# Layer 1's third and fourth PSUM bank as tiles of a pool of their own

## The chip, the core and the metric

The kernel runs on one core of a Trainium2 chip. A core has engines that work side by side, each through its own queue in order: TensorE (PE in the profile; its weight loads are PEld), VectorE (DVE), ScalarE (ACT), GpSimd (POOL) and SyncE (SP), which here issues transfers and reads a few values. TensorE writes its results to PSUM, a memory of eight banks of 128 partitions x 2 KB (512 float32 in each partition); VectorE and ScalarE read them from there into the larger memory SBUF. Engines wait for each other by semaphores, which the compiler of the kernel language sets: where a program takes a tile from a pool and writes it, the write waits until the readers of what lay there before are done.

The metric is the device time of one execution in microseconds (us), as the median of several runs.

## What is computed

Attention over windows (8 batches, 8 heads, 576 positions, 64 wide), and on its output a mixture of 16 experts in 4 groups. For each of 4,608 tokens one expert is chosen:

```python
x = attn_out.transpose(0, 2, 1, 3).reshape(B * S, H * D)     # 4608 x 512
g_idx = np.argmax(x @ w_group, axis=1)                       # group, then expert in the group
...
h = np.maximum(xg[mask_e] @ w1[g, e], 0.0)                   # layer 1: 512 -> 1024
ye = h @ w2[g, e]                                            # layer 2: 1024 -> 512
out[tok_idx] = combined[:, None] * ye
```

Inputs are float32. The change concerns the product `xg @ w1` of the experts, called layer 1 here.

## The kernel before, in words

The kernel works in two stages. Attention and the routing of tokens come first, in 36 steps of a hand-written software pipeline (the loop at L875). The experts follow, from some 184 us on. The order of the instructions on TensorE, ScalarE, VectorE and SyncE is the order of the program text (`manual_schedule`, L874); from L1057 on GpSimd's is too.

**Experts.** Experts are ranked by their number of tokens. Each gets a fixed number of slots (`CAPS`), split into pieces: three early pieces of 128, 128 and 256 slots, for which the tokens of the first batches suffice (the function `early`), and then 16 pieces, one per expert, of 192, 152, 368, 304, 304, 304, 296, 288, 272, 264, 256, 256, 248, 240, 216 and 192 slots (the loop at L1063). For each piece:

- *Gather and spread.* GpSimd gathers the rows of the piece's tokens (L690, tiles `xr`), one piece ahead. TensorE transposes them (`pt`, L721), ScalarE makes a float16 high part `xh` (L722) and VectorE the rest `xl` (L723). This runs between the matmuls of the piece before.
- *Layer 1* (`layer1`, L736). The 1,024 hidden columns are done in eight blocks of 128, `f` = 0 to 7. A block is 12 matmuls into one PSUM bank: 4 parts of the inner dimension, each with three products of float16 parts (weights high x `xh`, high x `xl`, low x `xh`). ScalarE then reads the bank and writes `hh`, the float16 of its positive part (L750), and VectorE reads the bank and writes the rest `hl` (L751).
- *Layer 2* (`layer2`, L759). For every 128 slots, 24 matmuls into a bank `y` (L802): for each of the eight blocks in order `hh` x high, `hl` x high, `hh` x low. In the middle of a tile stand transposes of the next piece. ScalarE scales the result (L776), GpSimd scatters it to the output (L763). A last tile of at most 64 slots is split into groups of columns; its slots are found by the small matmul `rp` (L666, after block 3), with VectorE's `entq` and ScalarE's `csq` behind it.
- *Weights.* The weights come as float32 in chunks of 512 KB through SyncE's queue (L611). ScalarE makes a chunk's high part (L625), VectorE its low part (L622). There are two sets of weights: while one expert works with one, the chunks of the next go into the other. Four chunks are done during layer 2 of a piece, the others during layer 1 of the following one, between the blocks, in the same queues of ScalarE and VectorE as `hh` and `hl`.
- Where no chunk is due, VectorE does a step of a table for tokens beyond the slots (`overflow`, tiles named `xT` in the profile), from 333 us to about 408 us.

**PSUM.** The eight banks are: psS with two tiles of one bank (attention's scores, later `a`), psT with two (transposes, `rp`), psA with one tile of two banks (attention's P times V, `o`), psX and psR with one bank each (layer 2's `y` in turn). Layer 1 takes its bank from `new_a` (L729). During attention that is always a psS tile. After attention (`att.close()`, L930) one last tile of two banks, `second`, is taken from psA and kept to the end (L942); the list `more_a` (L943) makes `new_a` give in turn the first half of `second`, a psS tile, the second half of `second`, a psS tile. So the even blocks of a piece write `second` and the odd ones `a`. A psS tile is handed out anew for every block; `second` is one tile for all blocks.

Of the kernel before, what the change touches and what calls it, by code (L numbers as in the profile page):

```python
# [8 lines left out]
F32 = mybir.dt.float32  # L9
# [6 lines left out]
PSUM = bass.MemoryType.PSUM  # L16

P = 128
# [46 lines left out]
def moe_attention_kernel(ctx, tc, q, k, v, cmask, wgate, wpack, out):  # L65
    nc = tc.nc
    pool = lambda name, bufs=1, **kw: ctx.enter_context(tc.tile_pool(name=name, bufs=bufs, **kw))
    cp = pool("cp")
    dram = pool("dram", space=bass.MemoryType.DRAM)
    psS = pool("psS", 2, space=PSUM)  # L70
    psT = pool("psT", 2, space=PSUM)
    psA = pool("psA", 1, space=PSUM)
    psX = pool("psX", 1, space=PSUM)
    psR = pool("psR", 1, space=PSUM)

# [19 lines left out]

    att = ExitStack()
    apool = lambda name, bufs=1, **kw: att.enter_context(tc.tile_pool(name=name, bufs=bufs, **kw))
    vp = apool("vp", NV)
    qp = apool("qp", NQ)
    kr = apool("kp").tile([P, 2, 2 * NK, 8, 32], F32, name="kr")  # L100
# [623 lines left out]
                xl[:, :, t * P : t * P + n], pt[:, :, 0:n], xh[:, :, t * P : t * P + n], ALU.subtract  # L724
            )

    more_a = []

    def new_a():  # L729
        if more_a:  # L730
            more_a.append(more_a.pop(0))
            if more_a[0] is not None:
                return more_a[0]
        return psS.tile([P, 512], F32, name="a", tag="s")

    def layer1(w, xs, cap, new_h):  # L736
        xh, xl = xs
        hh, hl = hs[:] = new_h()
        for f in range(8):
            a = new_a()  # L740
            mm = [(ww, xx, c) for c in range(4) for ww, xx in ((w[0], xh), (w[0], xl), (w[1], xh))]
            for i, (ww, xx, c) in enumerate(mm):
                nc.tensor.matmul(  # L743
                    a[:, 0:cap],
                    ww[:, c * FF + f * P : c * FF + f * P + P],
                    xx[:, c, 0:cap],
                    start=(i == 0),
                    stop=(i == len(mm) - 1),
                )
            nc.scalar.activation(hh[:, f, 0:cap], a[:, 0:cap], AF.Relu)  # L750
            nc.vector.scalar_tensor_tensor(  # L751
                hl[:, f, 0:cap], a[:, 0:cap], 0.0, hh[:, f, 0:cap], ALU.max, ALU.subtract
            )
            yield
# [184 lines left out]
    def new_h():  # L939
        return fh.tile([P, 8, CMAX], F16, name="hh"), fh.tile([P, 8, CMAX], F16, name="hl")  # L940

    second = psA.tile([P, 2, 512], F32, name="second", tag="o")  # L942
    more_a[:] = [None, second[:, 0], None, second[:, 1]]  # L943
    spare = xT[NBP - 1].rearrange("p c b i -> p (c b i)")
    taken = [0]

# [238 lines left out]
```

## Time and profile before

| | |
|---|---|
| median of 3 runs | 672.78 us (669.76 to 676.31) |
| the profiled execution | 663.49 us, of which the span from the first to the last instruction is 661.7 us |
| mean granted TensorE clock | 0.959 |
| busy share of the span | TensorE 89%, weight loads 62%, VectorE 61%, ScalarE 50%, GpSimd 38% |
| transfers | 127.53 MB, mean 193 GB/s |

By stages, the profile's windows say:

| us | what | TensorE busy | VectorE busy | ScalarE busy | clock | DMA share |
|---|---|---|---|---|---|---|
| 0 to 184 | attention | 147.90 | 135.19 | 98.35 | 0.94 | 0.75 |
| 184 to 234 | end of routing, early pieces | 40.91 | 25.12 | 21.55 | 0.83 | 0.25 |
| 234 to 272 | third early piece, first expert | 38.00 | 18.59 | 15.36 | 1.00 | 0.41 |
| 272 to 448 | the pieces of 152 to 296 slots | 160.60 | 111.62 | 86.74 | 0.98 | 0.62 |
| 448 to 573 | 288 to 256 slots | 120.70 | 72.95 | 69.75 | 0.99 | 0.66 |
| 573 to 662 | the last pieces | 80.03 | 41.97 | 39.84 | 0.98 | 0.43 |

How to read the rows of the profile: a row of the timeline has its start and its duration in us, the engine, the line of the kernel, the operation, what it writes `<-` what it reads, shapes, and in brackets how long its engine had been idle before it and what ended that (`<-`). `128*128 128x304` is a matmul with 128 x 128 weights and 304 columns. A row of the waits names the waiting engine and tile, what it waited for, the total in us, how often, and the longest. In the chain of waits each row has a start, a length and what it is; `x12` are twelve instructions merged. "issue" is idle time for which the profile shows no cause, "remote" the end of a wait whose origin it doesn't show.

### The profile page before, as it was taken

Reading aid. Unit: us, or ns where it says so; the run is one execution under the profiler, and the core shown is the slowest. Engines: PE = TensorE matmul, PEld = TensorE weight load, DVE = VectorE, ACT = ScalarE, POOL = GpSimd, SP = SyncE. Lnnn points to the kernel's source line nnn. Section 1 sums busy time; section 2 is a strip of 40 time slices with the busy share of each in tenths; the row PEclk is TensorE's granted clock in tenths of the full one; section 3 lists DMA queues with packets and bytes.
Section 4 is the critical chain, followed back from the end, with each engine's and each line's share of the span. In section 5 each row is a group of like instructions: output and inputs, shape, how many; then the busy total and the mean of one; then the engine's idle time right before and its main releaser. Section 6 shows DMA issues by size and latency. Waiting matters only on the chain.

```text
span 661.7 us, 18758 instructions
## 1 busy us (share of the span) xinstructions
PE 588.1 (89%) x7636; PEld 407.9 (62%) x7636; DVE 405.4 (61%) x849; ACT 331.6 (50%) x662; POOL 249.2 (38%) x304
## 2 busy tenths in 40 slices
PE   5898799878577999879989899898999999999896
PEld 4666576556464677655556566555576577667764
DVE  6765875887834672457485777554556567575720
ACT  2455565665532643456354455454557556556521
POOL 5874554539040171415142333414154134213311
PEclk9899989898796999979999999999999999999999
DMA  7887867796551026557565656656585677678300
GB/s 260 277 280 232 258 199 224 244 333 225 164 183 37 25 72 238 192 162 245 162 189 194 181 181 207 195 163 208 157 267 193 193 259 226 236 234 266 94 27 28
DMA packets 47916, 127.53 MB, mean 193 GB/s; under 512 B 7224, under 2 KB 8126, under 8 KB 47826
## 3 DMA queue, kind: packets, MB, share of 16 engines
q1 hardware_dynamic: 40466, 105.31, 50.0%
q0 software_dynamic: 7360, 20.98, 9.3%
q8 instruction: 62, 1.02, 0.6%
q14 instruction: 28, 0.23, 0.1%
HBM read 107.38 MB, written 19.24 MB: 191 GB/s over the span
## 4 chain that ended last, share of the span: by engine, by line
PE 57%; DVE 5%; issue 5%; ACT 3%; another core or an unknown queue 1%; POOL 0%; POOLq 0%; ACTq 0%
PE y L802 29%; PE second L743 12%; PE a L743 11%; PE pt L721 3%; DVE hl L751 1%; ACT hh L750 1%; PE lg_ps L389 1%; ACT wa1h L625 1%; ACT wa2h L625 1%; DVE wb1l L622 1%; PE lt_ps L378 0%; DVE wa1l L622 0%; DVE mv L492 0%; ACT wb2h L625 0%
## 5 line engine op out<-in xcount | busy, mean ns | idle before, releaser
L690 POOL DMA_INDIRECT xr<-xd,sent x80 | 96.5, 1206 | 33.2 <-issue 22.2
L763 POOL DMA_INDIRECT out<-yr,sent x30 | 30.0, 1001 | 204.6 <-ACT yr L776 180.8
L802 PEld LDWEIGHTS <-hh 128*128 128x128 f16 (+10 forms) x960 | 67.8, 99 | 59.8 <-issue 4.8
L743 PEld LDWEIGHTS <-wa1h 128*128 128x128 f16 x640 | 59.3, 98 | 25.7 <-issue 14.2
L723 DVE TENSOR_TENSOR xl<-pt,xh 128x512 f16<-128x512 f32 (+10 forms) x42 | 24.8, 595 | 77.7 <-ACT xh L722 69.0
L743 PEld LDWEIGHTS <-wb1h 128*128 128x128 f16 x576 | 55.9, 100 | 24.0 <-issue 13.2
L776 ACT ACTIVATE yr<-y,cs 128x512 f32<-128x512 f32 (+3 forms) x30 | 20.6, 688 | 91.7 <-PE y L802 67.4
L751 DVE SCALAR_TENSOR_TENSOR hl<-second,hh 128x256 f16<-128x256 f32 (+11 forms) x68 | 29.0, 427 | 55.6 <-ACT hh L750 41.4
L802 PE MATMUL y<-wb2h,hh 128*128 128x512 f16 (+6 forms) x272 | 60.6, 307 | 0.5 <-issue 0.5
L802 PE MATMUL y<-wb2h,hl 128*128 128x512 f16 (+6 forms) x272 | 60.4, 305 | 0.3
L802 PE MATMUL y<-wb2l,hh 128*128 128x512 f16 (+6 forms) x272 | 60.2, 305 | 0.5 <-issue 0.5
L802 PE MATMUL y<-wa2h,hl 128*128 128x512 f16 (+7 forms) x208 | 56.8, 330 | 0.1
L802 PE MATMUL y<-wa2h,hh 128*128 128x512 f16 (+7 forms) x208 | 56.9, 331 | 0.0
L127 POOL TENSOR_SCALAR vs<-vt 32x520 f32<-32x520 f32 x72 | 47.9, 665 | 23.8 <-DMA vt<-v 13.0
L802 PE MATMUL y<-wa2l,hh 128*128 128x512 f16 (+7 forms) x208 | 56.7, 330 | 0.0
L131 POOL TENSOR_SCALAR vs<-vt 32x520 f32<-32x520 f32 x64 | 41.9, 654 | 35.9 <-PE o L309 32.7
L802 PEld LDWEIGHTS <-hl 128*128 128x128 f16 (+10 forms) x480 | 35.0, 100 | 26.3 <-issue 1.2
L743 PE MATMUL second<-xh,wb1h 128*128 128x256 f16 (+6 forms) x144 | 39.6, 277 | 12.1 <-DVE hl L751 11.0
L750 ACT ACTIVATE hh<-a 128x256 f16<-128x256 f32 (+11 forms) x68 | 26.3, 387 | 42.9 <-PE a L743 22.0
L751 DVE SCALAR_TENSOR_TENSOR hl<-a,hh 128x256 f16<-128x256 f32 (+11 forms) x68 | 28.9, 425 | 30.1 <-ACT hh L750 19.2
L274 PE MATMUL s<-kr,qb 128*32 128x128 f32 x1152 | 43.3, 294 | 4.5 <-DMA kr<-k 2.2
L274 PEld LDWEIGHTS s<-kr,qb 128*32 128x32 f32 x1152 | 32.5, 117 | 18.0 <-issue 13.8
(201 smaller groups left out, 1552.5 us busy)
## 6 DMA issues: line engine op xcount, KB each, us to landing
w<-wpack SPq DMA_DIRECT2D x128, 512.0 KB
vt<-v SPq DMA_DIRECT2D x36, 260.0 KB
qb<-q SPq DMA_DIRECT2D x36, 256.0 KB
xd<-x SPq DMA_DIRECT2D x72, 128.0 KB
kr<-k SPq DMA_DIRECT2D x34, 256.0 KB
xr<-xd,sent POOLq DMA_INDIRECT x80
kr<-k SPq DMA_DIRECT2D x4, 128.0 KB
out<-yr,sent POOLq DMA_INDIRECT x30
```

What stands on the lines that cost most here:

```text
L127: nc.gpsimd.tensor_scalar(vs[n][even], vt[n][even], 1.0, 1.0, ALU.mult, ALU.mult)
L131: nc.gpsimd.tensor_scalar(vs[n][odd], vt[n - 1][odd], 1.0, 1.0, ALU.mult, ALU.mult)
L274: nc.tensor.matmul(s[32 * j : 32 * j + 32, c].rearrange("p w k -> p (w k)"), qv[:, (sl * 2 + a) * 32 : (sl * 2 + a) * 32 + 32], kr[:, :, k ...
L690: nc.gpsimd.indirect_dma_start(out=xr[:, 256 * h : 256 * h + 256], out_offset=None, in_=xd[0:known].rearrange("n (h c) -> (n h) c", h=2), ...
L721: nc.tensor.transpose(pt[:, c, 0:n], xr[0:n, c * P : c * P + P], id32[0:n, 0:n])
L723: nc.vector.tensor_tensor(xl[:, :, t * P : t * P + n], pt[:, :, 0:n], xh[:, :, t * P : t * P + n], ALU.subtract)
L743: nc.tensor.matmul(a[:, 0:cap], ww[:, c * FF + f * P : c * FF + f * P + P], xx[:, c, 0:cap], start=(i == 0), stop=(i == len(mm) - 1),)
L750: nc.scalar.activation(hh[:, f, 0:cap], a[:, 0:cap], AF.Relu)
L751: nc.vector.scalar_tensor_tensor(hl[:, f, 0:cap], a[:, 0:cap], 0.0, hh[:, f, 0:cap], ALU.max, ALU.subtract)
L763: ins = nc.gpsimd.indirect_dma_start(out=out.rearrange("n (g c) -> (n g) c", g=g), out_offset=bass.IndirectOffsetOnAxis(ap=at, axis=0), in ...
L776: nc.scalar.activation(yr[0:n, :], yp[0:n, :], AF.Copy, scale=cs[0:n, t : t + 1])
L802: nc.tensor.matmul(yp[P // g * j : P // g * j + n, 0 : DM // g], h[:, f, t * P : t * P + n], ww[:, f * DM + DM // g * j : f * DM + DM // g ...
```

## The change

psA becomes a pool of the attention stage (`apool`), so that its two banks are given back at `att.close()`. In its place a new pool psB is opened at that point, with two tiles of one bank each. `reuse_waits="tile"` lets a tile of the new pool wait only for the last use of the memory under that tile, as for the other pools opened there. `more_a` becomes a list of pools, and `new_a` takes a fresh tile in turn from psB and psS. The order of the four banks (psB, psS, psB, psS) is that of before, and no instruction is added to or taken from the text of an engine's work. In the profile the tiles of both pools are named `a`.

```diff
     psT = pool("psT", 2, space=PSUM)
-    psA = pool("psA", 1, space=PSUM)
     psX = pool("psX", 1, space=PSUM)
...
     apool = lambda name, bufs=1, **kw: att.enter_context(tc.tile_pool(name=name, bufs=bufs, **kw))
+    psA = apool("psA", 1, space=PSUM)
     vp = apool("vp", NV)
...
-    more_a = []
+    more_a = [psS]
 
     def new_a():
-        if more_a:
-            more_a.append(more_a.pop(0))
-            if more_a[0] is not None:
-                return more_a[0]
-        return psS.tile([P, 512], F32, name="a", tag="s")
+        more_a.append(more_a.pop(0))
+        return more_a[0].tile([P, 512], F32, name="a", tag="s")
...
-    second = psA.tile([P, 2, 512], F32, name="second", tag="o")
-    more_a[:] = [None, second[:, 0], None, second[:, 1]]
+    more_a[:] = [psS, pool("psB", 2, space=PSUM, reuse_waits="tile")]
```

## The prediction

> **What bounds the kernel now.** I read the chain of work first, then the waits of TensorE, then the timeline around those waits. The page gives span and chain:
>
> ```profile
> span 661.7 us, 18758 instructions
> PE 57%; DVE 5%; issue 5%; ACT 3%; another core or an unknown queue 1%; POOL 0%; POOLq 0%; ACTq 0%
> PE y L802 29%; PE second L743 12%; PE a L743 11%; PE pt L721 3%; DVE hl L751 1%; ACT hh L750 1%; PE lg_ps L389 1%; ACT wa1h L625 1%; ACT wa2h L625 1%; DVE wb1l L622 1%; PE lt_ps L378 0%; DVE wa1l L622 0%; DVE mv L492 0%; ACT wb2h L625 0%
> ```
>
> TensorE's matmuls of the expert layers (`second`, `a`, `y`) carry more than half of the chain, so a gap on TensorE there is time of the kernel. The view of waits, for PE alone, says which gaps there are (total us, times, longest):
>
> ```profile
> PE second L743 <- DVE hl L751: 18.9, 11, 4.8
> ...
> PE a L743 <- issue: 2.5, 3, 1.1
> ```
>
> The longest entry is layer 1 waiting to write a bank of `second` until VectorE has read one. `a`, the same matmuls into the other two banks, has no wait on VectorE or ScalarE in this list. The timeline of one of the eleven places, in the piece of 304 slots that begins at 360.6 us, shows which reader it waits for:
>
> ```profile
> 368.65 0.29 PE L743 MATMUL a<-xh,wa1h 128*128 128x304 f16 x1
> 368.95 0.42 ACT L750 ACTIVATE hh<-a 128x304 f16<-128x304 f32 x1 [3.10 <-PE second L743]
> 369.41 0.47 DVE L751 SCALAR_TENSOR_TENSOR hl<-a,hh 128x304 f16<-128x304 f32 x1 [1.77 <-issue]
> ...
> 370.07 0.29 PE L743 MATMUL a<-xh,wa1l 128*128 128x304 f16 x1
> ...
> 372.38 0.47 DVE L751 SCALAR_TENSOR_TENSOR hl<-second,hh 128x304 f16<-128x304 f32 x1 [0.67 <-ACT hh L750]
> ...
> 372.90 0.29 PE L743 MATMUL second<-xh,wa1h 128*128 128x304 f16 x1 [2.54 <-DVE hl L751]
> ...
> 376.00 0.38 PE L802 MATMUL y<-wa2h,hh 128*128 128x512 f16 x1
> ...
> 377.13 0.47 DVE L751 SCALAR_TENSOR_TENSOR hl<-a,hh 128x304 f16<-128x304 f32 x1
> ```
>
> Number the eight blocks of layer 1 f0 to f7: f0 and f4 write the first half of `second`, f2 and f6 the second half, the odd ones two psS tiles in turn. Block f6 starts at 372.90, 0.05 us after `hl` of f4 ended (372.38 + 0.47 = 372.85). But f4 used the other half; the last reader of f6's own half, `hl` of f2, was before all these rows. So a write to either half waits for the reads of both: `second` is two banks but behaves as one buffer that must be empty two blocks back. The psS tiles don't: f5 (`a`) starts at 368.65, before `hl` of f3 (the other psS tile) has even begun at 369.41.
>
> **The change part by part.**
>
> *Two tiles in place of two halves.* Each bank now has its own last reader, so a block waits for the `hl` four blocks back instead of two. In the piece above f6 then needs f2 only, and starts when f5 ends, at 370.07 + 0.29 = 370.36, so the whole 2.54 us goes. Block f7 needs f3's `hl`, done at 369.41 + 0.47 = 369.88, and does not wait either. The 11 waits together are 18.9 us. The largest of the others:
>
> ```profile
> 284.97 0.28 PE L743 MATMUL second<-xh,wb1h 128*128 128x152 f16 x1 [4.81 <-DVE hl L751]
> 342.77 0.29 PE L743 MATMUL second<-xh,wb1h 128*128 128x304 f16 x1 [2.60 <-DVE hl L751]
> 430.81 0.29 PE L743 MATMUL second<-xh,wa1h 128*128 128x296 f16 x1 [2.69 <-DVE hl L751]
> 461.09 0.40 PE L743 MATMUL second<-xh,wb1h 128*128 128x288 f16 x1 [3.14 <-DVE hl L751]
> ```
>
> *The clock.* The two longest waits cost more than their length. The chain in order of time (start, us, what) has the same work before and after them, and the windows their granted clock (behind the count of PE's instructions: PEclk, DMA share, GB/s):
>
> ```profile
> 273.22 0.79 PE second L743 x12
> 274.01 0.79 PE a L743 x12
> ...
> 284.97 1.68 PE second L743 x12
> 286.64 1.52 PE a L743 x12
> 288.16 3.53 PE y L802 x12
> 292.13 2.60 PE y L802 x12
> 448.68 1.47 PE second L743 x12
> 461.09 3.04 PE second L743 x12
> ```
>
> ```profile
> 284.97:288.16 3.19, 3.19 (x25) 0.50 0.58 189
> 461.09:465.61 4.52, 4.52 (x25) 0.68 0.79 226
> ```
>
> After the 4.81 us wait the clock is 0.50, and the work takes 1.68 + 1.52 + 3.53 - 0.79 - 0.79 - 2.60 = 2.55 us more; after the 3.14 us wait 3.04 - 1.47 = 1.57 us more. Without these pauses the clock stays up: 4.1 us.
>
> *What is late next.* ScalarE and VectorE don't become faster; TensorE only stops waiting for them there, and next meets their results in layer 2, which reads `hh` and `hl` block by block (three of its 24 matmuls for each, 2.60/12 = 0.217 us a matmul). In the 304 piece layer 2 starts 2.54 us earlier, at 373.5, and needs `hl` of f7 at its 23rd matmul, 373.5 + 22 x 0.217 = 378.2. VectorE has it at 377.13 + 0.47 = 377.6, even if it gains nothing: covered, by 0.6 us. The other places of the same size have the same order of work. The piece at 284.97 is short (152 slots) and not covered:
>
> ```profile
> 284.83 1.22 DVE L622 SCALAR_TENSOR_TENSOR wa2l<-w,wa2h 128x1024 f16<-128x1024 f32 x1
> ...
> 285.96 0.31 DVE L751 SCALAR_TENSOR_TENSOR hl<-a,hh 128x152 f16<-128x152 f32 x1
> ```
>
> Here `hl` of f5 ends at 285.96 + 0.31 = 286.27 and doesn't depend on f6. Behind them VectorE has `hl` of f6 (0.31), a weight chunk (1.22) and `hl` of f7 (0.31): 288.1. Layer 2's first tile then ends two matmuls later, at 288.6, and with the transposes in its middle (292.13 - 288.16 - 3.53 = 0.44) at 289.0; before it ended at 292.13 + 2.60 = 294.7. So this piece gains 5.7, not 4.81 + 2.55 = 7.4: 1.7 us come back as waits in layer 2.
>
> *Transfers and queues.* No DMA and no instruction of ScalarE, VectorE, GpSimd or SyncE is moved; all follow TensorE earlier. The pieces around the big waits use less of the DMA engines than later ones that run without a wait:
>
> ```profile
> 418.00:448.00 30.00, 27.31 (x210) 17.68 (x209) 15.48 (x30) 14.58 (x24) 9.07 (x9) 1.00 0.61 188
> 573.00:594.00 21.00, 21.00 (x151) 15.52 (x150) 13.72 (x24) 12.73 (x20) 6.81 (x6) 1.00 0.77 245
> ```
>
> 30 us shortened by 2.7 raises the share from 0.61 to 0.67, below the 0.77 at which TensorE is busy 21.00 of 21.00 us. Weights cost nothing more.
>
> *The pool's move.* PSUM still holds eight banks, and the new pool takes the two that attention gives back, at the point where `second` took them. Its first write waits for attention's last P times V result to be read, as `second` did: 0. Handing tiles over per block adds a release for some 76 blocks (half of 19 runs of layer 1 with 8 each). The psS tiles pay that already, and `a` has 2.5 us of issue idle in all, before 3 of its blocks: bounds 0 and 2.5; I take 0, as the other blocks of `a` show no gap.
>
> *Sum.* 18.9 + 4.1 - 1.7 = 21.3 us. The profiled execution took 663.5 us (span 661.7 and 1.8 around it), so it would take 642.2. The median of the runs, 672.8, lies 9.3 above it, and the trace doesn't show where; I carry the 21.3 us over unchanged: 651.5.
>
> That more buffering of results pays is not sure by itself. The Trainium skill, TensorE: Matmul & The Clock Gate, section HAM oscillation, tells of a kernel where PSUM double-buffering brought no further gain once the loop was in order. By that result the sum is 0 and the time 672.8; by the wait rows it is 21.3. I go by the rows, since there every wait ends 0.05 us after a read of the wrong bank; the rule's case is the first rival.
>
> **The rivals.**
>
> *The waits move into layer 2.* ScalarE and VectorE decide, and TensorE waits for `hl` of f4 to f7 at `y` instead. For it: the margin in the 304 piece is only 0.6 us, and the short piece already pays 1.7. Against it: by the sums above the large pieces are covered. It decides where `hl` of f7 comes over 0.6 us later than now. If half of the 21.3 comes back, the time is 672.8 - 10.7 = 662; if all of it, or if the new tiles still wait for each other, 672.8.
>
> *The late evacuations belong to this execution.* In the 304 piece ScalarE idles 3.10 us before `hh` of f3, though f3's matmuls had ended before 368.65, and no row says why. If other executions don't have this, the waits of 4.81, 2.54, 2.69 and 3.14 us (13.2) aren't there to be saved. Left are 18.9 - 13.2 = 5.7 us, of which the 2.60 has a visible cause: 672.8 - 5.7 gives 667. Against it: the four lie in four pieces, always before f6, and even the fastest run without the profile (669.8) took longer than the profiled one, not less.
>
> *The handover costs TensorE a bubble per block (slower).* If a released tile brings a second wait instruction before each of its blocks, all 76 of those blocks pay it. It turns the gain into a loss of 1% from (21.3 + 6.7)/76 = 0.37 us per block. At 0.4 us it gives 672.8 - 21.3 + 30.4 = 682. Against it: the `a` blocks are such tiles and show 2.5/76 = 0.03 us.
>
> **How the numbers follow.** One per cent, 6.7 us, is about what a measurement of this kernel can tell from no change. Forecast, all or nearly all of it: 0.62. Half of it returned in layer 2 (662): 0.13, also faster by over 1%. All returned, or no effect: 0.08; late evacuations not typical (667): 0.12; both within 1%. Handover: 0.05. So faster 0.75, same 0.20, slower 0.05. The likeliest gives 651.5. The runs' spread (669.8 to 676.3) is 3.3 us to each side, and the unexplained 9.3 us may hold some more such waits, half of it at most: 651.5 - 3.3 - 4.7 = 643.5. The range is 643 to 668: upwards it takes in the half return and the 667 of the second rival. The forecast alone: 645 to 657.
>
> **What the changed profile would show.** Right: no wait of the layer 1 matmuls on `hl` in TensorE's waits; the blocks f6 start at the end of f5; the clock at 1.00 around 285 and 461; one wait on `hl` at `y` L802 of under 2 us, in the 152 piece. Wrong: waits of `y` on `hl` or `hh` summing to over 5 us (first rival); `hh` of f3 and f4 prompt everywhere, or in other pieces (second); an issue gap before every block of the new tiles (third). The forecast fails as a whole if TensorE's idle time between 272 and 640 us stays what it is.

## The result, and the profile after

| | before | changed |
|---|---|---|
| median of 4 runs each | 671.27 us (666.93 to 676.31) | 649.69 us (649.06 to 653.69) |
| the profiled execution | 663.49 us | 649.06 us |
| mean granted TensorE clock | 0.959 | 0.963 |

The ratio is 0.969 (95% interval 0.961 to 0.977). The medians differ by 21.6 us, where 21.3 had been forecast, but the two profiled executions by 14.4 us only. So the sum fits the medians and is 7 us too large for the pair of traces that it was worked out from; where those 7 us are is the first question.

The page of the changed kernel, its span and the two rows of its chain:

```profile
span 647.3 us, 18720 instructions
PE 64%; issue 4%; DVE 1%; ACT 1%; POOL 0%; POOLq 0%
PE y L799 31%; PE a L740 29%; PE pt L721 3%; PE lg_ps L389 1%; PE lt_ps L378 0%; ACT off L246 0%; PE rp L666 0%; POOL out L760 0%; PE tb_ps L511 0%; DVE mv L492 0%; ACT ohl L247 0%; DVE x L334 0%; DVE room L723 0%; ACT yr L773 0%; ACT room 
```

VectorE's share of the chain falls from 5% to 1% and ScalarE's from 3% to 1%: the steps that ran over `hl` and `hh` are gone from it. TensorE's waits in the changed kernel (total us, times, longest):

```profile
PE a L740 <- issue: 9.9, 21, 1.0
...
PE y L799 <- issue: 1.3, 4, 0.5
```

Layer 1 (`a`, L740 now) has no wait on `hl`, and layer 2 (`y`, L799) none on `hh` or `hl`. In place of 18.9 us of waits on VectorE stand 9.9 us of "issue", where 2.5 (`a`) and 1.6 (`second`) stood before: TensorE stands still 21 times, and the profile shows no semaphore that holds it. By the timelines 2.4 of the 9.9 us lie in the first early piece, as 2.5 us did before. From the 152 piece on the changed kernel stops inside blocks for 7.5 us, the kernel before for 0.5.

The timeline of the piece of 304 slots whose waits the prediction used (from 355.27 us here) shows the wait gone although its cause is still there:

```profile
361.34 0.29 PE L740 MATMUL a<-xh,wa1l 128*128 128x304 f16 x1
361.57 0.28 PE L666 MATMUL rp<-tq,id 48*64 48x2 f32 x4
...
364.76 0.29 PE L740 MATMUL a<-xh,wa1l 128*128 128x304 f16 x1
364.89 0.29 PE L740 MATMUL a<-xh,wa1h 128*128 128x304 f16 x1
...
365.13 0.42 ACT L747 ACTIVATE hh<-a 128x304 f16<-128x304 f32 x1 [4.59 <-PE a L740]
...
366.56 0.30 PE L740 MATMUL a<-xh,wa1h 128*128 128x304 f16 x1 [0.43 <-issue]
...
368.24 0.47 DVE L748 SCALAR_TENSOR_TENSOR hl<-a,hh 128x304 f16<-128x304 f32 x1 [0.36 <-ACT hh L747]
```

Block f3 ends at 361.34 + 0.29 = 361.63, but ScalarE's `hh` of f3 starts at 365.13, 3.5 us later: by its row the wait ended with a signal of TensorE, so ScalarE is told late that TensorE is done. `hl` of f4 starts 12.97 us after the piece, even later than before (372.38 - 360.58 = 11.80). Yet f6 begins at 364.89, behind the last matmul of f5 at 364.76, without a gap. Then, inside f6, TensorE stops for 0.43 us, and the profile shows no cause.

The largest such stops are in the short piece of 152 slots. First TensorE, then GpSimd in the same time:

```profile
278.37 0.23 PE L740 MATMUL a<-xh,wb1h 128*128 128x152 f16 x1 [0.33 <-issue]
...
279.10 0.23 PE L740 MATMUL a<-xl,wb1h 128*128 128x152 f16 x1 [0.30 <-issue]
279.84 0.23 PE L740 MATMUL a<-xh,wb1l 128*128 128x152 f16 x1 [0.51 <-issue]
...
281.28 0.23 PE L740 MATMUL a<-xh,wb1h 128*128 128x152 f16 x1 [1.02 <-issue]
...
282.69 0.28 PE L740 MATMUL a<-xl,wb1h 128*128 128x152 f16 x1 [0.99 <-issue]
```

```profile
275.30 1.04 POOL L690 DMA_INDIRECT xr<-xd,sent  x1 [0.30 <-issue]
...
281.87 0.99 POOL L690 DMA_INDIRECT xr<-xd,sent  x1 [0.30 <-issue]
```

These are matmuls in the middle of a block, and they fall into the stretch (275.3 to 282.9 us) in which GpSimd issues six gathers, one every 1.3 us. From there on all of layer 1's stops lie within a piece's gathers or at most 1.3 us behind the last of them. The windows give the clock (third number from the end) in that stretch, behind its largest stops, in the piece of 288 slots, and behind the stops there:

```profile
276.00:288.00 12.00, 7.99 (x65) 5.05 (x63) 5.94 (x12) 4.46 (x11) 5.34 (x6) 0.73 0.65 196
284.00:288.00 4.00, 3.87 (x19) 2.49 (x20) 3.44 (x7) 2.75 (x6) 0.00 (x0) 0.50 0.70 184
440.00:450.00 10.00, 8.80 (x78) 6.61 (x76) 2.96 (x5) 3.07 (x6) 6.95 (x7) 1.00 0.59 191
449.99:454.50 4.51, 4.51 (x30) 2.86 (x30) 4.13 (x7) 4.21 (x8) 0.00 (x0) 1.00 0.45 132
```

Where the time came from is read from the starts of block f0 in the timelines, from one piece to the next:

| piece | before, us | changed, us | gain | forecast |
|---|---|---|---|---|
| 152 slots | 24.73 | 23.12 | 1.6 | 5.7 |
| 304, first of three | 30.20 | 27.43 | 2.8 | 2.6 |
| 304, second | 30.13 | 28.35 | 1.8 | 2.5 |
| 296 | 29.94 | 27.72 | 2.2 | 2.7 |
| 288 | 30.71 | 27.36 | 3.4 | 4.7 |
| 272 | 25.19 | 27.12 | -1.9 | 0 |
| from the start of 152 to the start of the last piece | 365.80 | 351.52 | 14.3 | 21.3 |

The missing 7.0 us are, to 0.3 us, the 152 piece (4.1), the 272 piece (1.9) and the 288 piece (1.3). The piece of 272 has three stops of this kind inside f6 (0.80, 0.20 and 0.43 us), the 288 one two (0.42 and 0.78).

### The profile page after: what moved, and what is told of

Read it like the earlier page. It is cut to its first block, busy times and chain, and to the rows that moved or that the text cites. A ratio compares the mean times of both kernels' runs of the same rounds, so it can differ in the third digit from the quotient of the medians.

```text
span 647.3 us, 18720 instructions
## 1 busy us (share of the span) xinstructions
PE 586.9 (91%) x7636; PEld 406.5 (63%) x7636; DVE 403.4 (62%) x849; ACT 330.2 (51%) x662; POOL 244.8 (38%) x304
## 4 chain that ended last, share of the span: by engine, by line
PE 64%; issue 4%; DVE 1%; ACT 1%; POOL 0%; POOLq 0%
PE y L799 31%; PE a L740 29%; PE pt L721 3%; PE lg_ps L389 1%; PE lt_ps L378 0%; ACT off L246 0%; PE rp L666 0%; POOL out L760 0%; PE tb_ps L511 0%; DVE mv L492 0%; ACT ohl L247 0%; DVE x L334 0%; DVE room L723 0%; ACT yr L773 0%; ACT room L747 0%
## 5 line engine op out<-in xcount | busy, mean ns | idle before, releaser
L748 DVE SCALAR_TENSOR_TENSOR hl<-a,hh 128x256 f16<-128x256 f32 (+11 forms) x136 | 57.2, 425 | 83.3 <-ACT hh L747 46.6
L690 POOL DMA_INDIRECT xr<-xd,sent x80 | 93.4, 1168 | 34.4 <-issue 21.9
L799 PEld LDWEIGHTS <-hh 128*128 128x128 f16 (+10 forms) x960 | 67.9, 99 | 59.8 <-issue 5.4
L747 ACT ACTIVATE hh<-a 128x256 f16<-128x256 f32 (+11 forms) x136 | 51.5, 386 | 67.5 <-PE a L740 54.8
L740 PE MATMUL a<-xh,wb1l 128*128 128x256 f16 (+6 forms) x288 | 77.8, 272 | 2.0 <-issue 2.0
L740 PE MATMUL a<-xl,wb1h 128*128 128x256 f16 (+6 forms) x288 | 77.8, 272 | 1.9 <-issue 1.9
L740 PE MATMUL a<-xh,wb1h 128*128 128x256 f16 (+6 forms) x288 | 77.8, 272 | 1.3 <-issue 1.3
L740 PEld LDWEIGHTS <-wa1h 128*128 128x128 f16 x640 | 59.9, 100 | 19.7 <-issue 8.4
L740 PE MATMUL a<-xh,wa1l 128*128 128x192 f16 (+7 forms) x256 | 71.1, 278 | 1.3 <-issue 1.0
L740 PE MATMUL a<-xh,wa1h 128*128 128x192 f16 (+7 forms) x256 | 71.2, 278 | 0.9 <-issue 0.9
L740 PE MATMUL a<-xl,wa1h 128*128 128x192 f16 (+7 forms) x256 | 71.1, 278 | 0.5 <-issue 0.5
L740 PEld LDWEIGHTS <-wb1h 128*128 128x128 f16 x576 | 54.9, 99 | 12.7 <-issue 2.8
L799 PE MATMUL y<-wb2h,hh 128*128 128x512 f16 (+6 forms) x272 | 60.6, 307 | 0.5 <-issue 0.5
L799 PE MATMUL y<-wb2l,hh 128*128 128x512 f16 (+6 forms) x272 | 60.5, 306 | 0.5 <-issue 0.5
L799 PE MATMUL y<-wb2h,hl 128*128 128x512 f16 (+6 forms) x272 | 60.6, 306 | 0.3 <-issue 0.2
L799 PE MATMUL y<-wa2h,hl 128*128 128x512 f16 (+7 forms) x208 | 56.8, 330 | 0.2 <-issue 0.2
L799 PE MATMUL y<-wa2h,hh 128*128 128x512 f16 (+7 forms) x208 | 56.9, 331 | 0.0
L799 PE MATMUL y<-wa2l,hh 128*128 128x512 f16 (+7 forms) x208 | 56.7, 330 | 0.0
L127 POOL TENSOR_SCALAR vs<-vt 32x520 f32<-32x520 f32 x72 | 47.6, 662 | 23.6 <-DMA vt<-v 12.5
```

The lines of the kernel that those rows point to most:

```text
L127: nc.gpsimd.tensor_scalar(vs[n][even], vt[n][even], 1.0, 1.0, ALU.mult, ALU.mult)
L690: nc.gpsimd.indirect_dma_start(out=xr[:, 256 * h : 256 * h + 256], out_offset=None, in_=xd[0:known].rearrange("n (h c) -> (n h) c", h=2), ...
L740: nc.tensor.matmul(a[:, 0:cap], ww[:, c * FF + f * P : c * FF + f * P + P], xx[:, c, 0:cap], start=(i == 0), stop=(i == len(mm) - 1),)
L748: nc.vector.scalar_tensor_tensor(hl[:, f, 0:cap], a[:, 0:cap], 0.0, hh[:, f, 0:cap], ALU.max, ALU.subtract)
L799: nc.tensor.matmul(yp[P // g * j : P // g * j + n, 0 : DM // g], h[:, f, t * P : t * P + n], ww[:, f * DM + DM // g * j : f * DM + DM // g ...
```

## The experiments

The theory: a write to either half of `second` waits for the reads of both, and separate tiles end that. The rivals were that the change of pool matters, that fresh tiles matter, that the number of banks matters, and later that the gain hangs on something outside the kernel's text. Twelve runs were made, in four series. Each ratio is to the kernel before in the same series; worked out over the runs, it can differ by up to 0.5% from the quotient of the medians shown here. Where an expectation speaks of a chip, read a series: the second and the third ran on the chip of the same number.

**What of the change matters (first series: the kernel before 636.87 us).** Four kernels take the change apart. In e1 and e2 the two lines that move psA to the attention stage are those of the change and aren't shown again.

`e1_two_lasting_tiles`: the two halves are separate tiles, taken once and kept, as `second` was.

```diff
-    second = psA.tile([P, 2, 512], F32, name="second", tag="o")
-    more_a[:] = [None, second[:, 0], None, second[:, 1]]
+    psB = pool("psB", 1, space=PSUM, reuse_waits="tile")
+    first_half = psB.tile([P, 512], F32, name="second", tag="h0")
+    second_half = psB.tile([P, 512], F32, name="second", tag="h1")
+    more_a[:] = [None, first_half, None, second_half]
```

> Two tiles of one bank each, taken once and kept for all blocks, in place of one tile of two banks; no fresh tile per block. Theory (the wait goes by the tile, whole): the waits of layer 1 on hl go as in the changed kernel, ratio 0.97 (0.96 to 0.98), and the list of TensorE's waits has no entry of layer 1 on hl above 1 us in total. Rival (a fresh tile for every block is what frees the bank): the 19 us of waits stay, ratio 0.99 to 1.01.

`e2_pool_moved_alone`: the pool's move, with one tile of two banks in it as before.

```diff
-    second = psA.tile([P, 2, 512], F32, name="second", tag="o")
+    psB = pool("psB", 1, space=PSUM, reuse_waits="tile")
+    second = psB.tile([P, 2, 512], F32, name="second", tag="o")
```

> The pool's move alone: attention's pool closes, and the new pool gives one tile of two banks that is used in halves as before. Theory: no gain, ratio 0.99 to 1.01, waits of second on hl 15 to 25 us in total. Rival (placement of the banks or the earlier release matters): ratio under 0.98.

`e3_psB_one_bank`: the changed kernel with one bank in the new pool; `e4_two_banks`: with none, so that layer 1 has psS's two banks only.

```diff
-    more_a[:] = [psS, pool("psB", 2, space=PSUM, reuse_waits="tile")]
+    more_a[:] = [psS, pool("psB", 1, space=PSUM, reuse_waits="tile")]   # e3
+    more_a[:] = [psS]                                                   # e4
```

> The changed kernel with one tile instead of two in the new pool: three banks in all, one left empty. An even block now waits for the even block two back, as before the change. Theory: the fourth bank of before was worth nothing, so ratio 0.99 to 1.01 and waits of even blocks on hl of 15 to 25 us. Rival (each bank counts for itself, by the room it gives): slower than before, ratio 1.02 or more.

> Layer 1 on the two psS banks alone: every block, odd ones too, waits for the one two back. Theory: the even blocks' waits stay as before (15 to 25 us) and the odd ones add where hl is late: in the trace of before block f5 would start 1.2 us later in the 304 piece, some 7 places, and part of that is taken off the f6 wait behind it: 0 to 8 us, ratio 1.00 to 1.015. Rival (two banks are too few at every block): each of 152 blocks pays some 0.2 us or more, ratio 1.04 or more.

| | us | ratio (95% interval) |
|---|---|---|
| e1 | 630.35 | 0.992 (0.988 to 0.996) |
| e2 | 634.01 | 1.000 (0.997 to 1.003) |
| e3 | 634.93 | 1.000 (0.996 to 1.004) |
| e4 | 637.00 | 1.002 (0.998 to 1.007) |

TensorE's waits of e2, e3 and e4, in this order; e1 has no wait of layer 1 on `hl`:

```profile
PE second L743 <- DVE hl L751: 5.1, 6, 2.2
```

```profile
PE a L740 <- DVE hl L748: 5.1, 6, 2.2
```

```profile
PE a L740 <- DVE hl L748: 5.5, 9, 1.7
```

e1 alone is faster, by 0.8%, as the theory has it, and the pool's move alone is worth nothing. But all sizes are far too small: e1 was expected at 0.97, and the waits of e2 to e4 at 15 to 25 us. In this series even the kernel before takes 637 us, and with `second` as one tile TensorE waits for `hl` 5.1 us instead of 18.9. Three banks or two bring no more than the time of before: a bank that waits for its neighbour is as good as none.

**Is it the wait? (Second series: before 675.58 us.)** Here the kernel before is as slow as at first. `e5_changed_again` is the changed kernel; `e6_before_late_hl` and `e7_changed_late_hl` put some 3 us of other work ahead of one `hl`, that of f4, in each of the 16 main pieces, in the kernel before and in the changed one.

```diff
             nc.scalar.activation(hh[:, f, 0:cap], a[:, 0:cap], AF.Relu)
+            if f == 4 and late_hl:
+                for _ in range(4):
+                    nc.vector.tensor_tensor(late_hl[0], late_hl[0], late_hl[0], ALU.max)
             nc.vector.scalar_tensor_tensor(
...
+    late_hl.append(spare[:, 4008:4608])
```

> The changed kernel once more, since on this chip the kernel before took 637 us and its copy showed only 5.1 us of waits of even blocks on hl. Theory (the change is worth the waits that the chip at hand has): 5 to 6 us, ratio 0.990 to 0.993, like the two lasting tiles. Rival (fresh tiles are worth more, as in the first comparison): ratio 0.97.

> The kernel before with four more VectorE operations on 600 numbers each (0.75 us each by the 576-wide operation in the trace, 3.0 us) put ahead of hl of block 4 in each of the 16 pieces. They leave values as they are. Theory: block 6 waits for hl of block 4; the slack now is the length of block 5 less the usual lag of hl, 0.3 to 0.8 us, so some 2.5 us in each piece, 16 x 2.5 = 40 us, ratio 1.05 to 1.07, waits of second on hl 35 to 48 us. Rival (VectorE is idle 38% of the time and takes it up, TensorE waits elsewhere at most): ratio under 1.02.

> The same four VectorE operations in the changed kernel. Theory: block 6 doesn't wait for block 4, and layer 2 needs hl late enough: 0 to 10 us over the changed kernel without them, ratio to the kernel before 0.99 to 1.01, no waits of layer 1 on hl. Rival (the wait only moves to layer 2): waits of y on hl or hh of 25 us or more, ratio 1.03 or more.

| | us | ratio (95% interval) |
|---|---|---|
| e5 | 648.35 | 0.960 (0.956 to 0.964) |
| e6 | 723.79 | 1.072 (1.067 to 1.077) |
| e7 | 653.33 | 0.966 (0.962 to 0.971) |

The added work of e6 by its group, and TensorE's wait in it:

```profile
L755 DVE TENSOR_TENSOR xT<-xT 128x600 f32<-128x600 f32 x64 | 50.0, 781 | 1.7
```

```profile
PE second L745 <- DVE hl L756: 60.4, 20, 6.7
```

And TensorE's waits in e7:

```profile
PE a L742 <- issue: 8.3, 16, 1.0
...
PE y L804 <- DVE hl L753: 3.8, 8, 0.9
```

e5 missed its expectation of 0.990 to 0.993, which had taken over the waits of the first series; its rival had 0.97. e7's ratio falls below the expected 0.99 for the same reason; the rest of e7's expectation came true. e6 came out a little above its 1.05 to 1.07, with 60.4 us of waits where 35 to 48 had been expected.

The same 50.0 us of VectorE's work cost 723.79 - 675.58 = 48.2 us with the tile of two banks and 653.33 - 648.35 = 5.0 us with two tiles. With the shared tile a late `hl` of f4 is a wait of f6, nearly one for one; with separate tiles it is a wait of `y` of at most 0.9 us.

**What makes the evacuations late?** In the profile before the five waits of 2.5 us and more all overlap GpSimd's gathers of the next piece's tokens. `e8_before_plain_rows` leaves out the gather by token: SyncE's queue loads as many plain rows instead. The eight gathers of the first early pieces (tiles `xe`) stay.

```diff
             xr = rows.tile([P, 512], F32, name="xr", bufs=4)
-            fetch_rows(xr, ent, t)
+            nc.sync.dma_start(xr, xd[t * P : t * P + P, :])
```

> The kernel before with the gather of GpSimd replaced by plain transfers of as many consecutive rows on SyncE's queue (the gather by token is left out, so the rows are those of other tokens). On a chip where TensorE's signals come late during the gathers: if the gathers are the cause, the waits of second on hl of 2.5 to 4.8 us at four pieces go, and the time falls by 10 us or more. If they aren't, or on a chip without the late signals, the time changes by under 5 us and the waits stay at about 5 us.

It ran in the second series and took 646.11 us (two runs), 0.956 (0.950 to 0.962) of the kernel before: 29 us less, with `second` still one tile. TensorE's wait, and then two rows of ScalarE's waits in it:

```profile
PE second L743 <- DVE hl L751: 3.7, 5, 2.2
```

```profile
ACT hh L750 <- PE a L743: 32.7, 41, 1.4
ACT hh L750 <- PE second L743: 21.2, 31, 1.4
```

Before, ScalarE's rows were these:

```profile
ACT hh L750 <- PE second L743: 38.9, 40, 3.2
ACT hh L750 <- PE a L743: 22.9, 32, 1.8
```

Without these gathers no `hh` waits more than 1.4 us for TensorE, and of the five long waits only that of the first piece of 304 slots (2.2 us) is still long. So it is the gathers, or what they load, that delay TensorE's signals to ScalarE; which part of a gather does it, no run shows.

**A third and a fourth series.** The third (before 633.66 us) had the changed kernel once more, the changed kernel with plain rows (`e9_changed_plain_rows`, the edit of e8 in the changed kernel), and an attempt to do better: `e10_changed_gather_later` issues the gathers of the next piece behind block f3 rather than ahead of f0.

```diff
-        if more:
-            nxt = begin(i + 1)
-            ncap = pieces[i + 1][2]
-            nc.gpsimd.drain()
...
+            if more and k == 3:
+                nxt = begin(i + 1)
+                nc.gpsimd.drain()
```

> The changed kernel with the gather of GpSimd replaced by plain transfers of consecutive rows on SyncE's queue (the gather by token is left out). Theory (GpSimd's gathers make TensorE's signals late, and where the banks no longer stop TensorE it stalls inside a block instead): on a chip where the kernel before takes 670 us or more, the idle time called issue in layer 1 from 270 us on (6 to 8 us in the changed kernel) goes, and the time is 6 to 10 us under the changed kernel's, ratio to before 0.94 to 0.955. On a chip where it takes 637 us: within 3 us of the changed kernel's. Rival (these stalls have to do with the fresh tiles): they stay.

> The changed kernel with the gather of the next piece started after block 3 of layer 1 instead of ahead of block 0. Theory: the late signals move with the gathers into blocks 4 to 7 and the first tile of layer 2, where hh and hl are needed sooner, so nothing is won: within 1% of the changed kernel, waits of y on hh or hl instead of the stalls inside a block. Rival (layer 2 doesn't mind late signals): 5 us or more faster than the changed kernel.

> The changed kernel beside the other two, for comparison on the same chip. If the kernel before takes 670 us or more: ratio 0.955 to 0.975 and 6 to 10 us of issue in layer 1. If it takes 637 us: ratio 0.988 to 0.995 and under 1 us of it.

The fourth (before 679.63 us) had e9's kernel again, since by its length it could tell more there:

> The changed kernel with plain rows in place of the gather by token (that gather is left out), once more. It serves if the kernel before takes some 670 to 676 us in this series, as in the series of e5 to e8. Theory (the gain beyond 0.5 to 0.8% is the gathers' late signals): with the plain rows the change is worth only what it is worth on a quiet chip, so the ratio to the kernel before is that of e8, 0.956, less 0.004 to 0.008: 0.948 to 0.952. Rival (the change saves its 3 to 4% whatever the gathers do): 0.956 x 0.965 = 0.923. Where the kernel before takes some 635 us both theories expect what e9 gave, 0.980 to 0.990, and nothing is told apart.

| | series' kernel before | us | ratio (95% interval) |
|---|---|---|---|
| e9, plain rows | 633.66 | 624.49 | 0.985 (0.980 to 0.990) |
| e10 | 633.66 | 656.18 | 1.037 (1.030 to 1.044) |
| e11, the changed kernel | 633.66 | 631.10 | 0.995 (0.992 to 0.999) |
| e12, plain rows | 679.63 | 637.92 | 0.937 (0.933 to 0.941) |

e11 is at the edge of its 0.988 to 0.995. e9 missed: it was expected within 3 us of e11 and is 6.6 us below it, so the gathers cost some 6 us even in a series without late signals, and not all of e8's 29 us is lateness. e10 missed too, 25 us above e11: the gathers come too late, and the transposes wait for them.

```profile
PE pt L721 <- DMA xr<-xd,sent: 21.3, 22, 2.1
```

e12 fell between the two numbers: the theory wanted 0.948 to 0.952, the rival 0.923. Against e8 it is 0.937/0.956 = 0.98, so by the medians the change is still worth 2% when the gathers are gone, not 0.4 to 0.8%. One part of the theory came out plainly in e12: of the 9.9 us of layer 1's stops in the changed profile this is left,

```profile
PE a L740 <- issue: 2.5, 6, 0.5
```

all six between 198 and 202 us, at the gathers of the early pieces, and none from the 152 piece on. The traces of e8 and e12 say more. From the start of the 152 piece to the start of the last one, by the first matmul of each f0:

| the series' kernel before, us | gathers | with `second` | with two tiles | difference |
|---|---|---|---|---|
| as in the profile before | by token | 365.80 (before) | 351.52 (after) | 14.3 |
| 675.58 (the kernel before has no trace there) | by token | 365.80 (the row above) | 349.35 (e5) | 16.5 |
| 675.58 and 679.63 | plain rows | 344.66 (e8) | 338.67 (e12) | 6.0 |
| 636.87 and 633.66 | by token | 345.56 (e2) | 339.70 (e11) | 5.9 |

Without the gathers the long series run this stretch as the short series run it with them, to 1 us, and there the change is worth 6 us instead of 14 to 16. (The short series without them, e9, takes 336.15, so 2.5 us of e12's 338.67 are still the long series'.) Much of the rest of the difference between the series lies in the first early piece: from its first matmul of layer 1 to that of the second it is 33.8 to 34.1 us in before, e5, e8 and e12 and 24.5 in e2 and e11. Its gathers no run leaves out. Of the 9.2 us between the spans of e8 (646.7) and e12 (637.5), the other 3.0 lie ahead of the 152 piece, most of them in attention, where the change does nothing. Whether the runs without a trace share that is not known, so e12's median stays unexplained by some 6 us.

## Why the prediction was right, and where its sizes were not

*Two tiles in place of two halves (18.9 us).* Right as a mechanism. The wait of layer 1 on `hl` is gone from after, e1, e5, e7 and e11 and present wherever the two banks are one tile or too few. Lasting tiles do it as well as fresh ones (e1, in a short series; in a long one they were not run). e6 and e7 show it by itself: 48.2 us against 5.0 for the same delay.

*The clock (4.1 us).* Right for one piece, wrong for the other. In the piece of 288 slots the clock stays at 1.00 behind the stops where it had fallen to 0.68. From 284 to 288 us it is 0.50, as low as before behind the wait, and not the 1.00 that was forecast; TensorE still pauses ahead of it. So the 2.55 us of this term that belong to the 152 piece are not seen to come.

*What is late next (1.7 us).* This is the term that was mis-sized. It looked for the loss in layer 2, as waits for `hl`; layer 2 has none. The loss is in layer 1 itself: stops of TensorE inside blocks, at the gathers, 7.5 us from the 152 piece on instead of 0.5. The 152 piece has 4.0 us of them and the low clock, and gains 1.6 instead of 5.7 us; the 272 piece has 1.4 us of them and loses 1.9. The wait on `hl` had covered part of the same stretches, and with it gone the next thing that holds TensorE there shows. The trace of before had the sign of it, and the prediction misread it. It took the 2.5 us of issue before `a` for idle time "before 3 of its blocks", an upper bound for a handover:

```profile
197.09 0.27 PE L743 MATMUL a<-room,wa1h 128*128 128x128 f16 x2 [1.07 <-issue]
198.52 0.27 PE L743 MATMUL a<-room,wa1l 128*128 128x128 f16 x1 [0.99 <-issue]
...
279.86 0.23 PE L743 MATMUL a<-xl,wb1h 128*128 128x152 f16 x1 [0.47 <-issue]
```

Counted from the start of their blocks these are the 4th, 9th and 11th of 12 matmuls: the stops are inside blocks, and each falls into a stretch of gathers or at most 1 us behind one.

*Transfers, queues and the pool's move (0).* Right: e2's ratio is 1.000 (0.997 to 1.003), no wait on a weight appears among TensorE's, and e11 has no "issue" entry for `a` at all, so a tile per block costs nothing that shows.

*The sum on the median (651.5).* It came out at 649.69, and that it came so close is partly luck. Between the profiled pair, from whose rows the sum was made, the change is worth 14.4 us. The other runs of before were longer than its profiled one (median 671.27 against 663.49), while those of the changed kernel hardly were (649.25 to 653.69 against 649.06). That these runs held more of the same waits fits the result; no trace of such a run exists, and it isn't shown.

*The rivals.* Waits moved into layer 2: no; they are absent from the changed profile, and even with 3.1 us of added delay per piece they come to 3.8 us (e7). A bubble per block: no (e11). "The late evacuations belong to this execution" was half right, and is the case to remember: they belong not to one execution but to a whole series. In the series of 637 us the four waits that it named are gone or down to 0.6 us, and 5.1 us are left in all where it said 5.7 (e2). There and in the series of 634 us the change is worth 0.5 to 0.8% (e11, and e1 in place of the changed kernel) instead of 3 to 4%.

*The rule weighed in the prediction.* The Trainium skill, TensorE: Matmul & The Clock Gate, section HAM oscillation, reports no further gain from PSUM double-buffering in its kernel. Here separate banks gave 0.960 to 0.995. Taken over to this kernel, that result comes near where the signals are prompt and misses by 22 to 27 us where they are late (the first comparison and e5).

## What to carry to other kernels

Give each PSUM bank that is filled and emptied by itself a tile of its own: a tile of two banks used in halves waits as one, and buys no more than if the second bank weren't there (e2 against e3, in a short series). A wait on a late reader shows that the reader is late, not why: look for what delays the reader's own signal (here the gathers), since what holds it may hold the next engine as soon as the wait is gone. And a size taken from one trace is a size for the conditions of that trace; the same two kernels differed by 4.0% in one series and by 0.5% in another, so a gain of this size wants more than one series.

## What the runs showed of the hardware

*Signals from TensorE can come microseconds late while GpSimd issues gathers.* In the changed kernel f3 ended at 361.63 and ScalarE was let go at 365.13. In e11, from a short series, the same gathers run and the signal is prompt:

```profile
350.31 0.29 PE L740 MATMUL a<-xh,wa1l 128*128 128x304 f16 x1
...
350.54 0.28 PE L666 MATMUL rp<-tq,id 48*64 48x2 f32 x4
...
350.64 0.42 ACT L747 ACTIVATE hh<-a 128x304 f16<-128x304 f32 x1 [1.13 <-PE a L740]
350.78 1.00 POOL L690 DMA_INDIRECT xr<-xd,sent  x1 [0.30 <-issue]
```

Here f3 ends at 350.31 + 0.29 = 350.60, and `hh` starts 0.04 us later, with a gather on each side. Leaving the gathers out took 29 us from the kernel before in a long series (e8) and 6.6 us from the changed kernel in a short one (e9 against e11).

*TensorE itself stands still in the same stretches*, in the middle of blocks; e12 without the gathers and e11 in a short series have no such stop in layer 1 from the 152 piece on. The starts after a stop lie about 0.72 us, or twice that, apart (278.37, 279.10, 279.84, 281.28, 282.69 above). The late starts of ScalarE and VectorE in the same piece keep nearly the same steps:

```profile
279.82 0.30 ACT L747 ACTIVATE hh<-a 128x152 f16<-128x152 f32 x1 [2.67 <-remote]
...
282.00 0.16 DVE L668 SCALAR_TENSOR_TENSOR entq<-rp,oob 128x1 int32<-128x1 f32 x1 [1.54 <-issue]
...
284.23 0.30 ACT L747 ACTIVATE hh<-a 128x152 f16<-128x152 f32 x1 [0.92 <-remote]
```

The first stands beside TensorE's 279.84, the second one step behind 281.28, the third about two steps behind 282.69. So one cause may hold all three engines; that isn't shown, and no run here tells a late signal from a late instruction.

*The same kernel took 634 to 680 us from one series to the next*, with no change of text, and each series agreed with itself within 2%. It isn't the chip alone: the series of 675.58 and of 633.66 us ran on the chip of the same number. What differs between them, whether the taking of the trace has a part in the late signals, and why the changed kernel's other runs hardly exceed its profiled one while those of before do, stays open.
